# Streaming and retrieval attention with a two-layer MLP: the first two w_in loads divided, and the head of the written order changed

## The chip, the cores and the metric

The kernel runs on one core of one Trainium2 chip. The metric is device microseconds of one execution, given as the median of several runs. One execution was also taken with the hardware profiler; all views of the trace are of that one.

## What is computed

Four batches, eight heads, 768 positions, head width 64. Heads 0, 2 and 6 see every earlier key (retrieval heads); the others see the first 4 keys and a window of 64 (streaming heads). The 3072 x 512 result goes through a product with w_in (512 x 2048), a leaky ramp with a slope per column, and a product with w_out (2048 x 512).

```python
scores = scale * np.matmul(q, k.transpose(0, 1, 3, 2))
...
scores = np.where(mask[None, :, :, :], scores, -1000000000.0)
scores = scores - np.max(scores, axis=-1, keepdims=True)
a = np.exp(scores)
a = a / (np.sum(a, axis=-1, keepdims=True) + 1e-09)
return np.matmul(a, v).astype(np.float32)
...
h = x @ w_in
g = np.maximum(h, 0.0) + alpha * np.minimum(h, 0.0)
return (g @ w_out).astype(np.float32)
```

## The kernel before

The work is cut into about 1200 named pieces. A list, ORDER, written out at the top of the file, gives the order in which the pieces are recorded. Each engine does its instructions in that order, and so do the two engines that ask for transfers: SP for the rows of q, k and v, POOL for the weights and most of the results. A piece that waits holds back everything behind it on its engine. Nothing is scheduled at run time.

Heads come in pairs, `PAIRS = [(2, 6), (1, 5), (0, 4), (3, 7)]`, and a pair of one batch is a segment n, 0 to 15. The names of a segment's pieces:

- Lq, Lk, Lv: the loads of its rows (lines 239, 253, 276 and, for the small tail of a streaming head's v, 281), on SP, into buffers that are used in turn. One load moves 0.39 MB in one to three transfers. A transfer also waits until the transfer eight places before it on these queues has landed.
- Cq, Ck, Cv: casts to bf16 (lines 350 and 354, 363, 385 and 390), for the first segments on POOL, which is also the engine that asks for the weights.
- Tq, Tk: six transposes each on PE (line 405, for the first half of segment 0 line 403); tq, tk: the copies out of PSUM, on ACT or DVE.
- S: a block of scores on PE (lines 455, 504, 543), s: its exponentials on ACT (L511 for retrieval heads, L565 for streaming heads), m: masks on DVE. The score blocks of the first four segments take turns on two pairs of PSUM banks, so a block waits for the exponentials of the block before last.
- A: probabilities times values on PE (line 594), a: division on DVE (lines 604 and 605); X, x: transposes and copies into xT, the input of the MLP.

The MLP goes over eight token ranges t. P is a block of the first product (line 639), p and g the ramp (lines 644 and 651), O and Q blocks of the second product (lines 659 and 717), D, Z and b the sums around them. For t = 0 the blocks P0.0 to P0.5 are cut in three by the input pairs: part 0 takes the pairs that segments 0 and 1 fill, part 1 the pair of segment 2, part 2 that of segment 3:

```python
for part, cs in enumerate((range(0, 2), range(2, 3), range(3, 4))):
    item(f"P0.{f}.{part}", P1, 0, f, cs, LEAD)
```

The weights are loaded by POOL, which casts on the way. wi0 to wi7 (line 818) each bring a quarter of the columns of w_in for 64 of the 128 partitions, all four input pairs; wi0 and wi1 hold the columns of P0.0 to P0.3, wi2 and wi3 those of f 4 to 7, and so on. wo0 to wo3 (line 822) bring w_out.

warm0 to warm8 are matmuls on a tile of zeros (line 813), 32, 3, 14 and otherwise 4 of them, that fill PE while it has nothing to do.

Of the kernel before, what the change touches and what calls it, by code (L numbers as in the profile page):

```python
# [83 lines left out]
def kernel(  # L84
# [138 lines left out]
    def dram(t, offset, dims):  # L223
        return bass.AP(t.tensor, t.offset + offset, dims)
# [66 lines left out]
    nmr = const.tile([128, 5, 144], bf16, name="nmr")  # L291
    nms = const.tile([128, 192], bf16, name="nms")
# [5 lines left out]
    w_in_b = wpool.tile([128, 4, d_ff], bf16, name="w_in_b")  # L298
# [23 lines left out]
    def item(name, fn, *args):  # L322
        I[name] = lambda: fn(*args)
# [367 lines left out]
    for t, u in UNITS:  # L691
# [3 lines left out]
        S1 = owns[UNITS.index((t, u)) % 2 if t >= 2 else 0]  # L695
# [114 lines left out]
    def warm(n):  # L810
# [2 lines left out]
            nc.tensor.matmul(bank(got[0])[:, 0:128], busy, busy, start=True, stop=True)  # L813
        give(got)

    def load_w_in(n):
        hh, lo = n % 2, n // 2 * 512
        nc.gpsimd.dma_start(w_in_b[D * hh:D * hh + D, :, lo:lo + 512],
                            dram(moe_w_in, 4 * D * hh * d_ff + lo, [[d_ff, D], [D * d_ff, 4], [1, 512]]))
# [6 lines left out]
    def fill(name, ap, value, eng=nc.vector):  # L826
        item(name, eng.memset, ap, value)
# [159 lines left out]
```

## Time and profile before

| | |
|---|---|
| median of 3 runs | 224.23 us (223.76 to 226.41) |
| the profiled execution | 225.82 us, span of its instructions 224.1 us |
| PE busy | 214.4 us, 96% of the span |
| DVE, ACT, POOL busy | 183.5, 145.4, 45.0 us |
| moved by DMA | 35.98 MB, 161 GB/s over the span |

Times in the trace count from the start of the span, in microseconds. A row of the timeline gives the start, the duration, the engine, the line, the operation, out and in, how many instructions are merged in the row, and in brackets how long the engine had been idle and what released it. Where a wait is for several things at once, the row names only the one that came last by the profile. A row of the busy time by stretch gives, after the stretch and its length, the busy time of PE, PEld, DVE, ACT and POOL with the number of instructions, the granted TensorE clock, the mean share of the DMA engines in use (over 1 where two queues overlap) and GB/s. A DMA queue's row gives packets, MB and the share of the time of 16 engines.

### The profile page before, as it was taken

The page shows a single profiled execution, that of the slowest core. Times are in us where ns is not written, and L with a number is a line of the kernel's source. Part 1 is how long each engine was busy: PE and PEld are TensorE (multiplying, and loading weights), DVE is VectorE, ACT ScalarE, POOL GpSimd, SP SyncE. Part 2 cuts the span into 40 slices and gives each one's busy share as a digit, 9 for nine tenths or more (in the row PEclk, how much of TensorE's full clock was granted, in tenths as well). Part 3 has the DMA queues.
Part 4 walks back from the last instruction along what each step waited for, and adds up shares of the span by engine and source line. Part 5 has one row for each costly group of instructions (what it writes and reads, how often), then busy time and mean ns, then how long its engine had stood idle before and what let it go on. Part 6 is the DMA issues. An engine that isn't in the chain of part 4 may idle for free.

```text
span 224.1 us, 5705 instructions
## 1 busy us (share of the span) xinstructions
PE 214.4 (96%) x2169; PEld 155.3 (69%) x2186; DVE 183.5 (82%) x464; ACT 145.4 (65%) x311; POOL 45.0 (20%) x90
## 2 busy tenths in 40 slices
PE   8889879999999999999999999999999999999993
PEld 7769755656556654557899757757889955588882
DVE  6859655978778769999999996999999847799761
ACT  5879547989888869677861346789784136653430
POOL 6659673250322010030001110020000010000000
PEclk9999999999999999999999999999999999999999
DMA  6999999999999999999993699686002431100034
GB/s 184 316 218 208 287 241 226 234 206 189 205 253 229 173 247 219 196 219 205 220 191 86 140 286 155 144 131 125 4 0 105 83 113 47 47 3 0 3 140 143
DMA packets 89624, 35.98 MB, mean 161 GB/s; under 512 B 76645, under 2 KB 87933, under 8 KB 89597
## 3 DMA queue, kind: packets, MB, share of 16 engines
q1 hardware_dynamic: 83484, 26.35, 57.2%
q0 software_dynamic: 5792, 8.93, 17.2%
q8 instruction: 17, 0.28, 0.5%
q10 hardware_dynamic: 320, 0.34, 0.5%
q14 instruction: 11, 0.08, 0.1%
HBM read 27.58 MB, written 6.29 MB: 151 GB/s over the span
## 4 chain that ended last, share of the span: by engine, by line
PE 72%; DVE 9%; DMA 8%; POOL 4%; issue 3%; ACT 2%; SPq 0%; DVEq 0%; POOLq 0%
PE P L639 33%; PE P L717 21%; PE P L659 8%; PE P L594 5%; DMA rows<-in_q_dram 4%; DMA rows<-in_k_dram 4%; DVE g L651 3%; PE P L472 2%; PE P L465 1%; DVE g L702 1%; ACT eR L511 1%; PE P L405 1%; DVE eR L521 1%; POOL g L363 1%; POOL vb L390 1%
## 5 line engine op out<-in xcount | busy, mean ns | idle before, releaser
L639 PE MATMUL P<-xT,w_in_b 128*128 128x256 bf16 (+1 forms) x501 | 87.8, 325 | 1.6 <-DVE xn L605 1.0
L651 DVE SCALAR_TENSOR_TENSOR g<-neg,oma,P 128x256 bf16<-128x256 f32 (+1 forms) x128 | 71.4, 608 | 14.3 <-ACT neg L644 13.8
L639 PEld LDWEIGHTS <-w_in_b 128*128 128x128 bf16 x512 | 48.9, 98 | 31.6 <-issue 1.7
L644 ACT ACTIVATE neg<-P 128x512 f32<-128x512 f32 x96 | 55.3, 606 | 22.0 <-PE P L639 11.5
L717 PEld LDWEIGHTS <-g 128*128 128x128 bf16 x432 | 41.4, 98 | 6.2 <-DVE g L702 0.2
L511 ACT ACTIVATE eR<-P 128x448 bf16<-128x448 f32 (+4 forms) x63 | 37.1, 627 | 4.2 <-PE P L504 2.6
L717 PE MATMUL P<-w_out_b,g 128*128 128x256 bf16 x288 | 35.5, 273 | 0.0
L735 POOL DMA_DIRECT2D out_dram<-ot x12 | 7.2, 604 | 88.3 <-ACT ot L759 31.0
L659 PE MATMUL P<-w_out_b,g 128*128 128x512 bf16 x90 | 22.6, 380 | 0.3
L559 ACT ACTIVATE eS<-P 128x352 bf16<-128x352 f32 x45 | 20.7, 492 | 2.7 <-PE P L472 1.7
L605 DVE TENSOR_TENSOR xn<-P,rcp 128x448 bf16<-128x448 f32 (+1 forms) x32 | 19.5, 608 | 1.1
L570 DVE TENSOR_TENSOR eS<-eS,ms_near 128x352 bf16<-128x352 bf16 x45 | 14.7, 335 | 0.5 <-ACT eS L559 0.4
L659 PEld LDWEIGHTS <-g 128*128 128x128 bf16 x96 | 8.6, 98 | 9.1 <-issue 0.8
L702 DVE TENSOR_TENSOR g<-g 128x1024 bf16<-128x1024 bf16 x18 | 12.3, 686 | 0.1
L521 DVE TENSOR_TENSOR eR<-eR,mr_near 128x128 bf16<-128x128 bf16 (+5 forms) x54 | 10.9, 225 | 1.4 <-ACT eR L511 1.4
L455 PE MATMUL P<-qT,kT 128*128 128x192 bf16 (+14 forms) x68 | 11.1, 251 | 0.2 <-ACT eS L565 0.2
L594 PEld LDWEIGHTS <-eS 128*128 128x128 bf16 x260 | 9.9, 97 | 1.8
L594 PE MATMUL P<-vb,eS 128*128 128x65 bf16 x260 | 10.7, 193 | 0.0
L472 PE MATMUL P<-qT,kT 64*128 64x176 bf16 (+11 forms) x160 | 10.6, 250 | 0.0
L472 PEld LDWEIGHTS <-kT 64*128 64x128 bf16 x160 | 6.5, 94 | 5.7 <-issue 5.1
L594 PE MATMUL P<-vb,eR 128*128 128x65 bf16 x276 | 10.1, 193 | 0.0
L594 PEld LDWEIGHTS <-eR 128*128 128x128 bf16 x276 | 9.5, 97 | 0.5
(125 smaller groups left out, 263.0 us busy)
## 6 DMA issues: line engine op xcount, KB each, us to landing
out_dram<-ot POOLq DMA_DIRECT2D x18, 256.0 KB, 3.5
rows<-in_k_dram SPq DMA_DIRECT2D x21, 192.0 KB
rows<-in_q_dram SPq DMA_DIRECT2D x18, 192.0 KB
rows<-in_v_dram SPq DMA_DIRECT2D x17, 192.0 KB
rows<-in_v_dram SPq DMA_DIRECT2D x14, 196.0 KB
rows<-in_q_dram SPq DMA_DIRECT2D x7, 384.0 KB
w_in_b<-in_moe_w_in_dram POOLq DMA_DIRECT2D x8, 256.0 KB, 10.1
w_out_b<-in_moe_w_out_dram POOLq DMA_DIRECT2D x4, 512.0 KB, 13.8
```

Of the source, the lines that this page charges most:

```text
L472: nc.tensor.matmul(to, keys[own], queries[own], start=True, stop=True)
L511: nc.scalar.activation(ebuf[n, hh][:, lo:hi].rearrange("p (x c) -> p x c", x=len(parts)), P[:, got[0]:got[0] + len(parts), 0:(hi - lo) // ...
L559: nc.scalar.activation(slots, sc[:, 0:352].rearrange("p (s c) -> p s c", c=176), AF.Exp, scale=scale)
L570: nc.vector.tensor_tensor(slots, slots, ms_near[:, 0:2, :] if m == 0 else ms_near[:, 1:3, :], op=ALU.mult)
L594: nc.tensor.matmul(pav[:, i, :], e[:, o:o + 128], vv[:, j, hh, 0:D + 1], start=(m == 0), stop=(m == len(terms) - 1))
L605: nc.vector.tensor_tensor(xn[n][:, 0:nt, D * hh:D * hh + D], pav[:, :, 0:D], rcp.to_broadcast([128, nt, D]), op=ALU.mult)
L639: nc.tensor.matmul(psg[:, w * i:w * (i + 1)], w_in_b[:, c, 128 * fb:128 * (fb + 1)], xT[:, c, o:o + w], start=(x == 0), stop=(x == 3))
L644: nc.scalar.activation(neg[t, f], bank(held["P", t, f][0]), AF.Relu, scale=-1.0)
L651: nc.vector.scalar_tensor_tensor(g_buf[t % 2][:, fb, 0:w], neg[t, f][:, c], oma[:, fb:fb + 1], bank(got[0])[:, c], op0=ALU.mult, op1=ALU.add)
L659: nc.tensor.matmul(bank(held["O", t, s][0]), g_buf[t % 2][:, f, 128 * s:128 * (s + 1)], w_out_b[:, f, :], start=(f == 0), stop=(f == 15))
L702: nc.vector.tensor_tensor(to, x0, x1, op=op)
L717: nc.tensor.matmul(q_bank(t, u, CHAIN[y]), left[t, u][y][:, f, :], right[y][:, f, :], start=(first and f == 0), stop=(f == 7), skip_group_ ...
```

## The change

wi0 and wi1 are each divided in two. Part a brings the input pairs 1 and 2 (those of segments 1 and 0), part b the pairs 0 and 3; together they bring the same bytes to the same place. The pieces from about the 21st to the 356th of ORDER stand in another order; the first 20 or so and everything from S4.0.2 on stand as before. No other piece is added or taken out. The instructions of PE are the same in number and kind.

What moves on the engines, as far as it is spoken of below:

- PE: the scores of segment 0 now follow Tk1 and Tq1; warm2 (14 matmuls) moves from behind Tk0.0 to ahead of S0.1.2; Tq2 and Tk2 no longer stand side by side; Tk4 moves ahead of Tq5, and Tq4 behind X3 and P0.1.1, P0.2.1, P0.0.1; Tk5 moves ahead of S4.0.5 and P0.11.
- SP: Lv1 moves ahead of Lk3, Lk4 ahead of Lq5, Lk5 and Lq7 ahead of Lk6 and Lq6.
- POOL: wi1a behind Ck0.1, then Ck2.0, Cv0, Ck2.1, then wi0a, wi1b and wi6 ahead of Cq2; wi0b between Ck3.0 and Ck3.1; wi7, wi5 and wi3 behind Cv2; Ck4.0 and Ck4.1 both ahead of Cq4; wo0 behind Ck5.0, then the mask near_r (nr), then Ck5.1, and the other w_out loads behind that.
- ACT: alpha's load (La) ahead of the first half of Lk0.

```diff
@@ -12,23 +12,23 @@
 ...
-busy zero id warm0 kz3 Lq0.0 sz1 vz2 nms nmr so1 vz0 Lq0.1 Lk1 warm8 warm5 warm3 kz1 qz0 one Lq1 Lk0 La Ck0.0 kz2
-Cq0.0 Tq0.0 tq0.0 Tk0.0 qz warm2 Lk2 kz0 tk0.0 Ck1.0 Ck1.1 Cq0.1 Tk1 S0.0.1 s0.0.1 Tq0.1 S0.0.0 Cq1 warm7 Lv0 tk1.0
-sz2 vz1 vz3 Tq1 Lq2 Ck0.1 S0.0.2 s0.0.0 tk1.1 Tk0.1 Ck2.1 tq1 S1.1.0 s0.0.2 Ck2.0 warm4 tq0.1 s1.1.0 Cq2 tk0.1 Cv0 Lk3
-S0.1.0 kfz0 Lv1 vo ro0 Ck3.1 s0.1.0 Lq3 Ck3.0 wi1 wi0 Cq3 sz0 idf S1.0.0 so2 Al s1.0.0 so0 al S0.1.1 s0.1.1 Lv2 Tq2
-Tk2 tk2.1 tk2.0 S0.1.2 S1.0.1 A0.0 s0.1.2 a0.0 Cv1 A0.1 a0.1 Cv2 s1.0.1 tq2 S1.1.1 Tk3 S2.0.1 tk3.0 s1.1.1 S2.0.2 X0
-s2.0.1 x0 wi6 s2.0.2 wi7 Lv3 Lq5 Tq3 tk3.1 S2.0.0 wi5 m4.0.2 warm6 S2.1.0 A1.0 a1.0 Lk4 tq3 A1.1 Cv3.0 s2.0.0 Lq4 Lk6
-Lq6 Lk5 wi4 Cq5 a1.1 S3.0.0 s2.1.0 A2.0 s3.0.0 X1 x1 S3.0.1 S3.1.1 Ck4.0 P0.2.0 s3.0.1 A3.0 a2.0 Lq7 a3.0 S2.1.1
-s3.1.1 wi2 s2.1.1 Cv3.1 S3.1.0 wi3 A2.1 Cq4 wo1 s3.1.0 P0.1.0 P0.3.0 A3.1 Lk7 P0.0.0 Tq5 a2.1 tq5 X2 a3.1 Ck4.1 X3 Tq4
-Lv5 tq4 Tk4 x2 P0.2.1 Lv6 P0.1.1 tk4.0 P0.3.1 P0.0.1 x3 tk4.1 P0.13 p0.13 P0.0.2 P0.1.2 wo0 p0.0 P0.3.2 g0.0 P0.14
-g0.13 P1.14 wo3 p0.1 p1.14 g0.1 P1.2 p1.2 P0.8 Lv4 g1.14 Ck6.0 P0.9 g1.2 Cq6 m8.0.2 p0.8 nr p0.9 g0.8 m12.1.2 p0.3
-near0 near2 P0.15 S4.0.5 p0.14 P1.10 s4.0.5 Ck6.1 P0.11 P0.2.2 g0.9 Ck5.1 g0.14 p0.15 p1.10 P1.0 Lq8 Tq6 ro1 Ck5.0
-g0.15 p0.2 g0.3 S4.1.0 g1.10 wo2 p0.11 P1.12 P1.8 P0.7 g0.2 Lk8 s4.1.0 kfz1 g0.11 Lk9 p1.0 P0.5.0 p1.12 tq6 g1.0
-P0.5.1 Tk5 P0.4.0 p1.8 P0.6 tk5.0 g1.12 Lv7 p0.6 P0.10 g1.8 g0.6 P0.12 S4.0.3 P0.4.1 tk5.1 Cq7 s4.0.3 P0.4.2 D1.0
...
+busy zero id warm0 kz3 Lq0.0 sz1 vz2 nms nmr so1 vz0 Lq0.1 Lk1 warm8 warm5 warm3 kz1 qz0 one Ck1.0 Lq1 La idf Ck1.1
+Lk0 Cq0.0 vz1 Ck0.0 Lk2 Tq0.0 Tk0.0 kz2 Cq0.1 vo kz0 m12.1.2 tq0.0 Cq1 tk0.0 Tk1 Ck0.1 Tq1 S0.0.0 qz Lv0 wi1a Ck2.0
+s0.0.0 Tq0.1 Al warm7 tq1 S0.0.1 Cv0 Lq2 s0.0.1 Lv1 tk1.0 S0.0.2 Ck2.1 wi0a tk1.1 Tk0.1 tq0.1 S1.1.0 tk0.1 wi1b Tk2
+s0.0.2 s1.1.0 Lk3 wi6 S0.1.0 warm6 S1.0.0 Lq3 tk2.1 Cq2 s0.1.0 s1.0.0 Cv1 S0.1.1 s0.1.1 sz2 warm2 ro0 S0.1.2 s0.1.2
+vz3 Tq2 tk2.0 Ck3.0 S1.0.1 A0.0 S1.1.1 s1.0.1 tq2 al sz0 wi0b A0.1 so0 a0.0 S2.0.1 Lv2 Ck3.1 Cq3 Cv2 warm4 a0.1 Tk3
+s1.1.1 S2.0.2 Lv3 s2.0.1 X0 Tq3 tk3.0 Lk4 s2.0.2 x0 tk3.1 Lq5 wi7 S2.0.0 A1.1 tq3 A1.0 S2.1.0 s2.0.0 S3.0.0 a1.0 wi5
+a1.1 A2.0 X1 Lq4 ro1 wi3 s2.1.0 x1 Lk5 s3.0.0 Cv3.0 S3.0.1 Lq7 a2.0 Lk6 Lq6 S3.1.1 P0.3.0 s3.0.1 S2.1.1 A3.0 wi4 Cv3.1
+so2 a3.0 s3.1.1 Cq5 Ck4.0 S3.1.0 Ck4.1 P0.1.0 s2.1.1 A2.1 a2.1 m4.1.2 s3.1.0 m8.0.2 P0.2.0 A3.1 kfz2 P0.0.0 wi2 Cq4
+Lk7 X2 Tk4 a3.1 Tq5 x2 near0 X3 near2 tk4.0 tk4.1 Ck5.0 P0.1.1 P0.2.1 Lv6 Lv4 Lv5 P0.0.1 x3 Tq4 P0.1.2 P0.13 wo0 Lq8
+nr P0.0.2 tq5 tq4 P0.3.1 p0.1 P0.3.2 P0.14 Ck5.1 kfz1 p0.0 P0.2.2 P1.2 p0.14 g0.0 P1.14 Tk5 g0.1 g0.14 p0.13 S4.0.5
+wo2 P0.11 p1.2 g1.2 p0.3 tk5.0 p1.14 P1.0 g0.3 s4.0.5 p0.11 P0.9 g1.14 P0.8 g0.13 tk5.1 g0.11 p0.9 P1.10 S4.1.0 wo1
+P0.7 g0.9 p0.2 P0.15 p0.8 Lk8 p1.0 s4.1.0 wo3 g0.2 g0.8 P0.5.0 p1.10 g1.0 p0.15 Lv7 g1.10 P0.10 ns S5.1.1 g0.15 P1.12
+P0.4.0 S4.0.1 near1 m4.1.0 p0.7 P0.4.1 s5.1.1 p0.10 D1.0 S4.1.3 p1.12 P0.4.2 s4.0.1 g0.7 p0.4 P1.8 g1.12 m4.0.1 kfz0
+g0.4 p1.8 m4.0.2 g0.10 Ck6.1 Lk9 S5.1.2 P0.5.1 P0.12 s5.1.2 m5.1.2 P0.6 S5.0.1 p0.12 P0.5.2 s4.1.3 O0.1.0 p0.6 Cq7
...
@@ -813,6 +813,11 @@
             nc.tensor.matmul(bank(got[0])[:, 0:128], busy, busy, start=True, stop=True)
         give(got)
 
+    def load_w_half(n, part):
+        first = (1, 0)[part]
+        nc.gpsimd.dma_start(w_in_b[D * n:D * n + D, first:4 - first:(1, 3)[part], 0:512],
+                            dram(moe_w_in, (4 * n + first) * D * d_ff, [[d_ff, D], [(1, 3)[part] * D * d_ff, 2], [1, 512]]))
+
     def load_w_in(n):
         hh, lo = n % 2, n // 2 * 512
         nc.gpsimd.dma_start(w_in_b[D * hh:D * hh + D, :, lo:lo + 512],
@@ -861,7 +866,11 @@
         item(f"near{i}", to_near, i)
     for i in range(4):
         for x in range(i, 8, 4):
-            item(f"wi{x}", load_w_in, x)
+            if x < 2:
+                for part in range(2):
+                    item(f"wi{x}{'ab'[part]}", load_w_half, x, part)
+            else:
+                item(f"wi{x}", load_w_in, x)
         item(f"wo{i}", load_w_out, i)
         fill(f"kfz{i}", kf[i][:, 6, :, :], 0.0, nc.gpsimd)
     fill("nz0", NATK[0].bitcast(fp32), 0.0, nc.gpsimd)
```

More of the change, by code (lines that the diff above doesn't have):

```diff
@@ L25 @@
-near0 near2 P0.15 S4.0.5 p0.14 P1.10 s4.0.5 Ck6.1 P0.11 P0.2.2 g0.9 Ck5.1 g0.14 p0.15 p1.10 P1.0 Lq8 Tq6 ro1 Ck5.0
-g0.15 p0.2 g0.3 S4.1.0 g1.10 wo2 p0.11 P1.12 P1.8 P0.7 g0.2 Lk8 s4.1.0 kfz1 g0.11 Lk9 p1.0 P0.5.0 p1.12 tq6 g1.0
-P0.5.1 Tk5 P0.4.0 p1.8 P0.6 tk5.0 g1.12 Lv7 p0.6 P0.10 g1.8 g0.6 P0.12 S4.0.3 P0.4.1 tk5.1 Cq7 s4.0.3 P0.4.2 D1.0
-p0.10 D1.1 P0.5.2 S4.0.1 p0.5 O0.0.0 g0.10 P1.4 s4.0.1 P1.6 p0.4 near1 g0.5 g0.4 S4.1.3 p0.7 p1.6 m4.0.3 g0.7 s4.1.3
-p1.4 O0.1.0 g1.6 O0.0.1 S5.1.2 ns S4.0.0 g1.4 O0.1.1 p0.12 s5.1.2 g0.12 S4.1.1 S5.0.1 m5.1.2 s4.0.0 m4.0.1 S5.0.0
@@ L30 @@
-S4.1.4 S5.1.1 S4.0.4 O0.0.2 s5.0.1 s4.0.4 Cv6 S5.1.0 S5.0.2 Ck7.1 s4.1.4 m4.0.0 s5.1.1 Tk6 O0.2.0 m4.1.0 Cv5 kfz2
-tk6.1 O0.0.3 O0.1.2 Ck7.0 s5.1.0 m5.1.1 O0.1.3 m4.1.2 Cq8 m5.0.1 s5.0.0 Ck8 tk6.0 Cv4 m5.1.0 O0.2.1 m5.0.0 o0.0 S4.0.2
+busy zero id warm0 kz3 Lq0.0 sz1 vz2 nms nmr so1 vz0 Lq0.1 Lk1 warm8 warm5 warm3 kz1 qz0 one Ck1.0 Lq1 La idf Ck1.1
+Lk0 Cq0.0 vz1 Ck0.0 Lk2 Tq0.0 Tk0.0 kz2 Cq0.1 vo kz0 m12.1.2 tq0.0 Cq1 tk0.0 Tk1 Ck0.1 Tq1 S0.0.0 qz Lv0 wi1a Ck2.0
+s0.0.0 Tq0.1 Al warm7 tq1 S0.0.1 Cv0 Lq2 s0.0.1 Lv1 tk1.0 S0.0.2 Ck2.1 wi0a tk1.1 Tk0.1 tq0.1 S1.1.0 tk0.1 wi1b Tk2
@@ L32 @@
+g0.4 p1.8 m4.0.2 g0.10 Ck6.1 Lk9 S5.1.2 P0.5.1 P0.12 s5.1.2 m5.1.2 P0.6 S5.0.1 p0.12 P0.5.2 s4.1.3 O0.1.0 p0.6 Cq7
+P1.6 Ck6.0 s5.0.1 g0.6 Cv4 S5.0.0 Tk6 Ck7.0 p0.5 g0.12 O0.0.0 p1.6 Cq6 g1.8 P1.4 g0.5 s5.0.0 Ck7.1 tk6.1 O0.0.1 Tq6
+S5.1.0 tq6 S4.0.0 O0.1.1 g1.6 s5.1.0 O0.0.2 Cv6 tk6.0 m5.1.1 p1.4 Cq8 S4.0.3 S4.1.1 S4.0.4 S4.1.4 O0.0.3 s4.0.4 S5.0.2
+O0.1.2 s4.1.4 D1.1 s4.0.3 s4.0.0 m5.0.1 O0.1.3 m4.0.3 g1.4 Cv5 m4.0.0 Ck8 O0.2.0 m5.1.0 O0.2.1 m5.0.0 o0.0 S4.0.2
 S6.0.2 m4.1.4 S4.1.5 S6.1.0 s4.1.1 S6.0.5 o0.1 S6.1.2 m4.0.5 s5.0.2 S4.1.2 s4.0.2 s4.1.5 D2.1 s6.1.0 Lq9 O0.2.2 m4.0.4
```

## The prediction

> **What bounds the kernel now.** I read the page's engine totals and its chain first, then the busy time by stretch, then each wait of PE ahead of 35 us, then what those waits hang on.
>
> ```profile
> PE 214.4 (96%) x2169; PEld 155.3 (69%) x2186; DVE 183.5 (82%) x464; ACT 145.4 (65%) x311; POOL 45.0 (20%) x90
> PEclk9999999999999999999999999999999999999999
> PE 72%; DVE 9%; DMA 8%; POOL 4%; issue 3%; ACT 2%; SPq 0%; DVEq 0%; POOLq 0%
> ```
> ```profile
> 5.00:10.00 5.00, 4.58 (x66) 3.85 (x66) 4.16 (x12) 4.00 (x5) 3.26 (x7) 1.00 1.11 304
> 10.00:15.00 5.00, 3.86 (x44) 3.04 (x44) 2.91 (x12) 4.38 (x6) 1.77 (x3) 1.00 0.96 233
> 25.00:30.00 5.00, 4.16 (x67) 3.48 (x70) 3.67 (x9) 1.75 (x4) 3.89 (x7) 1.00 1.16 275
> 30.00:35.00 5.00, 3.51 (x37) 2.23 (x35) 1.23 (x3) 3.17 (x4) 4.26 (x6) 1.00 1.18 240
> 100.00:150.00 50.00, 49.79 (x494) 36.96 (x497) 47.52 (x113) 30.27 (x73) 4.22 (x7) 1.00 0.89 174
> 200.00:224.10 24.10, 20.45 (x187) 17.88 (x184) 15.94 (x34) 7.16 (x20) 0.00 (x0) 1.00 0.18 66
> ```
> PE is the bound: full from 35 us to 200 us, with room only in the head and in the tail. The tail's pieces keep their order, and the change adds no PE instruction. So whatever it does is decided by PE's waits in the first 35 us, and by new ones behind them. These are the old ones:
>
> ```profile
> 6.87 0.51 PE L405 MATMUL P<-ident,g 128*128 128x128 bf16 x6 [0.18 <-POOL g L363]
> 10.23 0.49 PE L405 MATMUL P<-ident,g 128*128 128x128 bf16 x6 [0.47 <-DVE kT L436]
> 12.28 0.24 PE L455 MATMUL P<-qT,kT 128*128 128x192 bf16 x1 [0.16 <-ACT eS L565]
> 14.55 0.84 PE L405 MATMUL P<-ident,g 128*128 128x128 bf16 x12 [0.75 <-POOL g L350]
> 25.78 0.38 PE L639 MATMUL P<-xT,w_in_b 128*128 128x512 bf16 x1 [0.96 <-DVE xn L605]
> 31.63 0.51 PE L405 MATMUL P<-ident,natq 128*128 128x128 bf16 x6 [0.77 <-POOL natq L350]
> 32.85 0.51 PE L405 MATMUL P<-ident,natk 128*128 128x128 bf16 x6 [0.72 <-POOL natk L363]
> ```
> They add up to 4.0 us. Even if all of them went and nothing new came, the time would fall by 4.0 of 224.2 us, under the 2% that a measurement of this kernel can about tell from no change.
>
> **The change part by part.** Sums go against the profiled execution's 225.82 us (span 224.1), 1.59 us above the median of the runs; I move the result by that.
>
> *Scores begin later: +1.05 us at PE.* In the new order PE makes Tk1, then Tq1, and only then the first score block S0.0.0; warm2, which filled the place, stands later.
>
> ```profile
> 7.71 0.83 POOL L350 CAST g<-rows 128x768 bf16<-128x768 f32 x1 [0.44 <-DMA rows<-in_q_dram]
> 8.48 0.39 PE L813 MATMUL P<-busy 128*128 128x128 bf16 x4
> 8.70 0.50 PE L405 MATMUL P<-ident,g 128*128 128x128 bf16 x6
> 9.04 0.35 PE L455 MATMUL P<-qT,kT 128*128 128x128 bf16 x2
> 7.99 0.35 PE L455 MATMUL P<-qT,kT 128*128 128x448 bf16 x1
> 7.85 1.75 ACT L511 ACTIVATE eR<-P 128x896 bf16<-128x896 f32 x2 [1.00 <-PE P L504]
> 15.99 0.92 ACT L511 ACTIVATE eR<-P 128x896 bf16<-128x896 f32 x1 [1.23 <-PE P L504]
> ```
> Tq1 needs the cast that ends at 7.71+0.83 = 8.54. Six transposes hold PE 9.04-8.70 = 0.34, a block of S0 8.48-7.99 = 0.49 and a drain of about 0.1, so the first exponentials start at about 9.5 instead of 7.85: ACT is 1.65 late. From there to s0.1.2 ACT has the same nine instructions; before, it had 1.23 of wait and more among them (s0.1.2 ends at 15.99+0.92 = 16.9), in the new order I count 0.5, so it ends at 17.4. PE's S0.1.2 ends at about 16.5 (S0.1.1 at 15.15, warm2's fourteen at 0.056, then 0.55) against 15.79. Tq2 (0.34) and warm4 (0.22) are then still to do, warm6 (0.22) is done: 0.71+0.34+0.22-0.22 = +1.05. Bounds 0.5 (ACT recovers all it can) to 1.65.
>
> *Three waits go: -2.9 us.* 0.96 for the first weights, 0.77 for Tq4, 0.72 for Tk4, and with each about 0.16, since a transpose's record lasts 0.22 where the next follows after 0.056.
>
> ```profile
> L818 POOL DMA_DIRECT2D w_in_b<-in_moe_w_in_dram x2: 642/708/773, 16.4 to 17.1; - x2
> DMA to landing us min/median/max: 6.6/7.4/8.3
> 30.74 0.83 POOL L350 CAST natq<-rows 128x768 bf16<-128x768 f32 x1 [1.64 <-DMA rows<-in_q_dram]
> 31.51 0.77 POOL L822 DMA_DIRECT2D w_out_b<-in_moe_w_out_dram x1
> 32.28 0.52 POOL L363 CAST natk<-rows 128x384 bf16<-128x384 f32 x1
> ```
> The second weight load was asked for at 17.1 and lands 8.3 later, at 25.4, the matmul runs at 25.78: the row names DVE, but the weights fit. Asked for at about 9 and 12.5, the halves with pairs 1 and 2 are there long before the first L639, now P0.3.0 at about 25.5 to 27. Tk4 waited on POOL because Ck4.1 stood behind Cq4's wait and a w_out issue; now it stands ahead of both. Tq4 now follows Tk4 and three more matmuls (1.0 us of work), and by the sum of the pieces is reached at 31.6 if nothing else is late, just when a cast like the old one (30.74+0.83) ends.
>
> *The weights take the rows' engines: +1.6 us, bounds 0 and 2.6.*
>
> ```profile
> q1 hardware_dynamic: 4503, 2.43, 111.2%
> q0 software_dynamic: 1172, 1.13, 74.5%
> q1 hardware_dynamic: 1167, 1.00, 42.8%
> 10.77 3.16 SPq L281 DMA_DIRECT2D rows<-in_v_dram x1
> 13.97 0.38 SPq L239 DMA_DIRECT2D rows<-in_q_dram x1
> 15.46 0.96 POOL L363 CAST g<-rows 128x384 bf16<-128x384 f32 x2
> 17.74 0.85 POOL L350 CAST g<-rows 128x768 bf16<-128x768 f32 x1
> ```
> The first line is the queue view of 5 to 13 us, rows alone: 304 KB per us. The next two are of 27 to 36 us, weights beside them: the packets go one for one (1172 to 1167), and the rows fall to 111 KB per us while a weight load of 0.26 MB takes 2.1 us. So a weight load ahead of a row transfer costs it 2.1 x (1-111/304) = 1.3 us, a half 0.65. Now k3: before, it was issued ahead of the blocked SP instruction (L281, until 13.93) and cast at 15.46 to 16.4 with no wait. Now Lv1 with that L281 stands ahead of Lk3, and wi1a, wi0a, wi1b and wi6 are asked for before about 14.3. Lower bound: k3 lands by the old rate, one row load (1.3) and three halves (1.95) later, 18.7, one cast 19.2, in time for Tk3, which the order reaches at 19.5: 0. Upper: it is issued as q3 was (13.97, cast at 17.74, 3.8 later), plus two and a half weight loads 3.3, so 21.0, second cast 21.6: 2.1; with q3 behind it 0.5 more. I take 1.6, nearer the upper, since k3 really stands behind the L281.
>
> *k5: +0.4 us, bounds 0 and 1.5.* Tk5 moves up to about 4.5 us behind Tq4 (some 38 us); k5 is now the load behind q4, and its second cast stands behind a w_out issue (0.77) and the mask near_r (1.28). Beside the weights its 0.39 MB take 3.5 us more than q4: about 38. That cover gone, DVE and the POOL issues behind Ck5 are late too.
>
> *Priced at nothing.* Two more weight issues on POOL (0.64 each) come by 14.3, ahead of Cq2; Tq2 is wanted only at 16.5 now. That is also why the 0.75 wait of Tq2 does not return; it is contained in the 1.05. alpha's DMA ahead of Lk0 on ACT delays the k0 cast by 0.45, behind Tq0.0's six transposes. Lk2 waits as much longer, but SP soon blocks at Lq2 anyway. From 35 us on the same work is reordered under a full PE; w_out is asked for later, but its first user, the P2 block, comes at 52 us.
>
> Sum: +1.05 -2.9 +1.6 +0.4 = +0.15, taken as +0.2: 226.0 of span and launch, **224.4 us** beside the median: no change.
>
> **The rivals.** *Rows in time (faster, 222.4).* k3 and k5 are on time, both terms 0: 1.05-2.9 = -1.85. For it: the old DMA engines had a hole that early weights can fill for nothing:
>
> ```profile
> 14.00:15.40 1.40, 0.85 (x14) 0.84 (x15) 0.00 (x0) 0.76 (x1) 1.40 (x3) 1.00 0.46 57
> ```
> Against: k3's place behind L281.
>
> *q4 starved (slower, 227.2).* Its load took 9.88 us already.
>
> ```profile
> 20.81 9.88 DMA rows<-in_q_dram
> ```
> The weight queue starts some 7 us earlier and can by then have moved 7 x 0.126 = 0.88 MB more, 3.4 loads at 1.3 = 4.4 us: q4 lands at 35.1, its cast ends at 35.95 and Tq4 starts 4.35 after its 31.6. That takes k3's place in the sum: 1.05-2.9+4.35+0.4 = +2.9. It decides once q4 lands after about 32.3. Against: the last five weight loads stand behind Cv2 and Cv3.0 in POOL's order as before, so they start no earlier.
>
> *The first weights were not the wait (225.5).* Then DVE's xn was, 0.96+0.16 stay: +1.1. Against: xn was done at 25.5, and nothing of P0 reads it.
>
> *PE's clock falls back (225.9).* From the last warm matmul at about 5 us to S0.0.0 at 8.9 PE has only 24 transposes. If the clock halved, some 2 us of matmuls would double, about 1.5 us of it not hidden behind ACT. Against:
>
> ```profile
> 29.70:33.20 3.50, 2.01 (x34) 1.67 (x32) 1.53 (x3) 1.60 (x2) 2.46 (x4) 1.00 1.17 241
> 33.20 1.03 PE L639 MATMUL P<-xT,w_in_b 128*128 128x512 bf16 x4
> ```
> Here PE made transposes alone for 3.5 us, 2.01 of it busy, and the four matmuls after it stand (1.03-0.38)/3 = 0.22 apart, full rate. [...]
>
> **How the numbers follow.** Forecast (223.3 to 225.9) 0.42; rows in time 0.22; q4 starved 0.20; weights not the wait 0.10; clock 0.06. The likeliest is 224.4. The range takes the first rival's centre at the low end and the second's at the high end: 222.2 to 227.3. Faster by over 2% (below 219.7) needs more than all old waits together: 0.02. Slower by over 2% (above 228.7) is the far half of the starved case with a further stall behind it: 0.08. Within: 0.90.
>
> **What would show it.** Right: first L511 on ACT at about 9.5; no wait ahead of the first L639; a wait of PE of 1 to 2 us at the transposes near 20 us, released by POOL's L363 behind a k row; none or a short one for Tq4; a short one at about 38 us. If PE's idle time ahead of 35 us is under 2.5 us, the rows were in time; if the longest wait is for natq near 33 us, q4 was starved; if L813 or the scores at 9 us run at half rate, the clock. A new PE wait behind 40 us, where I count none, makes the prediction wrong, as does a first L639 that still waits.

## The result: a little slower, by 1%

The changed kernel takes 227.41 us (median of 22 runs, 225.5 to 229.62) beside 225.21 us for the kernel before on the same chip (22 runs). The ratio is 1.0096, 95% interval 1.0072 to 1.012: about 2.2 us were lost, where the forecast had +0.2, and 227.41 lies just above its range of 222.2 to 227.3. The loss is under 2% and clear of the noise. Medians are of all executions of a kernel, and ratios leave out those more than 1.5% above its fastest, so the two can differ a little. (The forecast's 224.4 stood beside 224.23, the median of the first three executions of the kernel before.)

The first profiled execution of the changed kernel took 228.96 us and had a lower granted clock (mean 0.992), so the readings below are from another execution of the same kernel, 227.04 us, clock 1.00 throughout (the run c_again). It stands beside the profiled execution of the kernel before, 225.82 us, so this pair of traces shows 1.2 us of the loss. Its page, engine totals, clock and the shares of the chain:

```profile
PE 215.0 (95%) x2169; PEld 155.5 (69%) x2186; DVE 183.1 (81%) x464; ACT 145.7 (65%) x311; POOL 47.1 (21%) x92
PEclk9999999999999999999999999999999999999999
PE 69%; DMA 12%; DVE 9%; SPq 3%; issue 2%; ACT 2%; POOL 2%; ACTq 0%; DVEq 0%; POOLq 0%
```

PE has the same 2169 instructions. Its share of the chain fell from 72% to 69% and the share of the DMA engines rose from 8% to 12%. Its waits of 0.15 us and more ahead of 45 us, from its timeline:

```profile
5.72 0.52 PE L403 MATMUL P<-ident,g 128*64 128x128 bf16 x6 [0.24 <-ACT g L363]
6.97 0.51 PE L405 MATMUL P<-ident,g 128*128 128x128 bf16 x6 [0.72 <-POOL g L363]
8.85 0.51 PE L405 MATMUL P<-ident,g 128*128 128x128 bf16 x6 [1.37 <-POOL g L350]
10.86 0.54 PE L455 MATMUL P<-qT,kT 128*128 128x448 bf16 x3 [0.18 <-ACT eR L511]
20.18 0.51 PE L405 MATMUL P<-ident,g 128*128 128x128 bf16 x6 [0.17 <-POOL g L363]
24.88 0.97 PE L594 MATMUL P<-vb,eR 128*128 128x65 bf16 x27 [0.25 <-POOL vb L390]
28.13 0.49 PE L594 MATMUL P<-vb,eS 128*128 128x65 bf16 x11 [0.26 <-POOL vb L341]
39.89 4.51 PE L639 MATMUL P<-xT,w_in_b 128*128 128x512 bf16 x27 [1.01 <-DMA w_in_b<-in_moe_w_in_dram]
```

They add up to 4.2 us; the seven of before made 4.0. The three that the forecast struck out are gone: the first L639 (26.99), Tk4 and Tq4 (31.59 to 33.3) start without a wait. In their place stand a longer head, two short waits for values and 1.01 us for weights at 39.89, at a place where before had none. The chain of the same run says where that one comes from:

```profile
12.59 0.47 SPq L276
13.11 10.68 DMA rows<-in_v_dram
23.89 0.95 POOL vb L390
25.80 1.23 POOL w_in_b L823 x2
27.03 0.57 POOL vb L385
28.03 11.81 DMA w_in_b<-in_moe_w_in_dram
39.89 0.39 PE P L639
```

Read downwards: SP asks for v2 at 12.59, sooner than in the kernel before (14.40), but the second of its transfers takes 10.68 us, with weights asked for ahead of it (the first at 9.19) and beside it (the last at 13.86); POOL stands 2.85 us at the cast Cv2, until 23.89; behind Cv2 in POOL's order are the last five weight loads, asked for from 25.2 on; the fourth of them, wi4, is asked for at 28.03 and lands at 39.85, and PE waits for it at P0.11. In the kernel before the same cast ran at 20.11 and the same issues at 21.39:

```profile
20.11 0.92 POOL L390 CAST vb<-rows 128x896 bf16<-128x896 f32 x1
21.39 1.84 POOL L818 DMA_DIRECT2D w_in_b<-in_moe_w_in_dram  x3
```

So asking for the first weights 7 us earlier made the cast of v2 3.8 us later and with it four of the last five weight loads (wi4 28.03 against 26.06). The order of the loads counts as well. The kernel before asks for wi4 ahead of wi2 and wi3; wi4 lands at 36.18, 2.0 us ahead of P0.8 (38.18), the first block that needs it. The changed order asks for wi3 ahead of wi4, although P0.7, the first block that needs wi3, comes 4.5 us behind P0.11 (44.43; wi3 landed at 37.62). Meanwhile SP, which loads the rows, stood 5.45 us at the issue of v3 in the changed kernel, against 1.32 us before:

```profile
16.90 5.45 SPq L276 DMA_DIRECT2D rows<-in_v_dram  x2
```

and the DMA engines were not kept full. Busy time by stretch, 20 to 25 us, the last two columns being the share of the DMA engines and GB/s, the changed kernel:

```profile
20.00:25.00 5.00, 4.58 (x79) 4.17 (x79) 4.31 (x12) 4.34 (x6) 2.00 (x4) 1.00 0.81 167
```

and the kernel before:

```profile
20.00:25.00 5.00, 4.82 (x97) 4.56 (x95) 3.88 (x11) 4.00 (x7) 3.17 (x6) 1.00 1.15 230
```

### The profile page after: what moved, and what is told of

Its sections match the earlier page's. It is cut to its first block, busy times and chain, and to the rows that moved or that the text cites. A ratio compares the mean times of both kernels' runs of the same rounds, so it can differ in the third digit from the quotient of the medians.

```text
span 227.2 us, 5709 instructions
## 1 busy us (share of the span) xinstructions
PE 217.0 (96%) x2169; PEld 157.3 (69%) x2186; DVE 183.1 (81%) x464; ACT 145.6 (64%) x311; POOL 46.5 (20%) x92
## 4 chain that ended last, share of the span: by engine, by line
PE 66%; DMA 13%; DVE 9%; SPq 6%; issue 2%; POOL 2%; ACT 0%; ACTq 0%; DVEq 0%; POOLq 0%
PE P L639 30%; PE P L717 21%; PE P L659 7%; DMA w_in_b<-in_moe_w_in_dram 5%; DMA rows<-in_v_dram 4%; PE P L594 4%; SPq L276 3%; DVE g L651 3%; DMA xT<-xn 2%; PE P L472 2%; DMA rows<-in_k_dram 2%; PE P L465 1%; SPq L239 1%; DVE g L702 1%; DVE eR L521 1%
## 5 line engine op out<-in xcount | busy, mean ns | idle before, releaser
L639 PE MATMUL P<-xT,w_in_b 128*128 128x256 bf16 (+1 forms) x501 | 88.7, 325 | 1.9 <-DMA w_in_b<-in_moe_w_in_dram 1.3
L651 DVE SCALAR_TENSOR_TENSOR g<-neg,oma,P 128x512 bf16<-128x512 f32 (+1 forms) x128 | 71.8, 608 | 12.8 <-ACT neg L644 11.9
L639 PEld LDWEIGHTS <-w_in_b 128*128 128x128 bf16 x512 | 48.8, 98 | 32.2 <-DMA w_in_b<-in_moe_w_in_dram 1.6
L455 PE MATMUL P<-qT,kT 128*128 128x192 bf16 (+14 forms) x68 | 12.0, 262 | 0.2
L472 PE MATMUL P<-qT,kT 64*128 64x176 bf16 (+10 forms) x156 | 10.4, 251 | 0.4 <-DMA kT<-natk 0.4
```

Source lines behind the costliest of these rows:

```text
L472: nc.tensor.matmul(to, keys[own], queries[own], start=True, stop=True)
L639: nc.tensor.matmul(psg[:, w * i:w * (i + 1)], w_in_b[:, c, 128 * fb:128 * (fb + 1)], xT[:, c, o:o + w], start=(x == 0), stop=(x == 3))
L651: nc.vector.scalar_tensor_tensor(g_buf[t % 2][:, fb, 0:w], neg[t, f][:, c], oma[:, fb:fb + 1], bank(got[0])[:, c], op0=ALU.mult, op1=ALU.add)
```

## The experiments

Ratios are to the kernel before, timed on the same chip, with 95% intervals. The edits move names in ORDER and nothing else, except where a run says otherwise.

**The changed kernel again**, twice, for traces.

> The changed kernel, unaltered, for a second trace. Three causes are in dispute. Late scores: the first exponentials on ACT start about 3 us later than before (11.05 against 7.85), about 2 us of which stays. Late weights: the early weight halves delay v2 (24.6 against 19.1 us), so POOL asks for the last five weight loads 3 to 4 us later and PE waits 1.3 us at 41 us. Clock: PE idles 2 us ahead of the first scores and the granted clock falls to 0.50 from 9.4 to 12.7 us, 1.7 us of clock lost. If the clock is the cause, an execution with the clock at 1.00 throughout is about as fast as before (ratio 1.00); if the other two are, it stays at 1.009 to 1.010 and the wait at 41 us is there with the clock at 1.00 too.

Measured: 226.95 us (12 runs), ratio 1.0081 [1.0054, 1.0109]. The clock fell in this trace too (to 0.50, from 8.9 to 12.3 us) and its span was still only 225.0 us; wi4 landed at 37.87 and PE came to P0.11 at 39.46, so that it did not wait for weights. Over 34 executions of the changed kernel the mean clock was under 0.995 in 7, over 95 of the kernel before in 16; the medians of the others are 227.15 and 225.22 us. The clock is not the difference.

> The changed kernel, unaltered, for a third trace, since the second one showed no wait at 41 us. Late weights: v2 lands at 22 us or later again and the waits that follow differ from run to run (values at 27 to 30 us, natk or natq at 33 to 35, weights at 38 to 41), 0.3 to 2.8 us together; time 226.5 to 227.8. If the early weights did nothing, v2 would land by 20 us and no such wait would be there.

Measured: 227.04 us with the clock at 1.00, the trace shown above. The 1.01 and 0.51 us of new waits are in the expected range.

**Scores first.**

```diff
-Tk1 Ck0.1 Tq1 S0.0.0 qz Lv0
+Tk1 Ck0.1 S0.0.0 Tq1 qz Lv0
```

> The transposes of q1 stand behind the first score block S0.0.0 instead of ahead of it; all else as in the changed kernel. Late scores: the first exponentials start at about 8.4 us instead of 11.05, and 1.5 to 2 us of the loss comes back: ratio to before 1.000 to 1.003. Late weights: the wait at 41 us is still there, grows by what PE gained ahead of it, and the ratio stays at 1.008 to 1.010. Clock: PE's longest idle stretch ahead of 10 us shrinks from 1.25 to about 0.9 us; if that keeps the clock at 1.00, ratio 1.003 in runs that had it low and no change in the others.

Measured: 227.26 us, 1.0089 [1.0056, 1.0122]. The first exponentials came at 8.81 us, 1.1 earlier than in c_again, and no gain can be measured: in the trace PE stands at P0.11 for 0.50 us, until 38.26, and wi4 lands at 38.22. The late scores are not the cause.

**Weights late.**

```diff
-... wi1a Ck2.0 ... wi0a ... wi1b ... wi6 ... wi0b ... Ck3.1 Cq3 Cv2 ... wi7
+... Ck2.0 ... Ck3.1 wi1a wi1b wi0a wi0b Cq3 Cv2 ... wi6 wi7
```

> The changed kernel with the four halves asked for together behind Ck3.1 and the third weight load behind Cv2, about where the kernel before asks for its first two and its third. Late weights: v2 and v3 land by about 20 and 25 us, the wait at 41 us (1.34) and the one for the values at 29 us (0.26) go, but the first L639 may wait up to 1 us for its weights again; ratio 1.003 to 1.007. Late scores: nothing of the 2 us comes back, ratio 1.008 to 1.012 (the more if the first weights are waited for).

Measured: 225.52 us, 1.0017 [0.9991, 1.0043]. Five weight transfers moved back on POOL take away most of the loss: 1.4 us less than the changed kernel in the same comparison. The ratio lies a little below the range of the first reading. The stretch of 20 to 25 us is full again:

```profile
20.00:25.00 5.00, 5.00 (x101) 4.62 (x99) 4.58 (x13) 4.69 (x6) 4.87 (x10) 1.00 1.03 227
```

and the chain reaches the weights sooner, the cast of v2 at 20.26 and the wait at their end 0.23 us (chain, then timeline):

```profile
20.26 0.87 POOL vb L390
21.54 2.41 POOL w_in_b L823 x4
24.87 12.85 DMA w_in_b<-in_moe_w_in_dram
37.76 0.39 PE P L639
37.76 4.51 PE L639 MATMUL P<-xT,w_in_b 128*128 128x512 bf16 x27 [0.23 <-DMA w_in_b<-in_moe_w_in_dram]
```

**Filler into the hole.**

```diff
-Tk1 Ck0.1 Tq1 ... S0.1.1 s0.1.1 sz2 warm2
+Tk1 Ck0.1 warm2 Tq1 ... S0.1.1 s0.1.1 sz2
```

> The changed kernel with the fourteen warm-up matmuls of warm2 moved from behind S0.1.1 to between the transposes of k1 and of q1, into PE's idle stretch of 8 to 9.2 us. Clock: the granted clock stays at 1.00 in every run, the mean falls to the level of the runs with clock 1.00, ratio 1.005 to 1.008 (about 227.4 less 0.3 to 1.0). Late scores: PE is held at most 0.1 us longer ahead of Tq1, and the removed filler at 17 us stood under ACT's work: ratio 1.009 to 1.010. Late weights: the same, the wait at 41 us stays.

Measured: 227.78 us, 1.011 [1.0066, 1.0155]; mean clock 0.999 or 1.0 in all six executions. That is a little above the ranges given; with the clock up in all of them nothing was gained.

**Both: weights late and scores first.**

> The changed kernel with both edits of the first runs: the halves asked for behind Ck3.1 and the third weight load behind Cv2, and the first score block ahead of the transposes of q1. Late weights alone: the same as with the weights alone put back, ratio 1.000 to 1.003, because the head's lateness was never the bound. Late scores as well: with the transfers on time the first exponentials at 8.4 instead of about 9.5 us now count, and 0.7 to 1.5 us come back: ratio 0.995 to 0.998.

Measured: 226.14 us, 1.0037 [1.0003, 1.0071], above both forecast ranges. Again nothing from the scores. PE stood 0.66 us at the transposes of k2 at 12.8 instead, which led to the two runs at the end of this section.

**The other five weights ahead of Cv2.**

```diff
-Ck3.1 Cq3 Cv2 ... wi7 ... wi5 ... wi3 ... wi4 ... wi2
+Ck3.1 Cq3 wi7 wi5 wi3 wi4 wi2 Cv2
```

> The changed kernel with the last five weight loads (wi7, wi5, wi3, wi4, wi2) asked for ahead of the cast of v2, while POOL waits for v2's rows; the early ones stay early. If the harm of the early weights goes by POOL's order (v2 late, so the last weights late, so PE waits for them at 37 to 41 us), these now land by about 36 us, no L639 waits for them, and the ratio falls to 1.002 to 1.005. If it goes by the rows themselves (every row load behind a weight is late: the values for L594, then k4 and q4), v2 and v3 land later still, PE waits for vb and for natk or natq, and the ratio rises to 1.012 to 1.025.

Measured: 231.59 us, 1.0188 [1.0119, 1.0257]. Of the two readings the second held. PE no longer waits for weights; it waits for rows:

```profile
28.80 0.22 PE L594 MATMUL P<-vb,eS 128*128 128x65 bf16 x2 [1.43 <-POOL vb L385]
34.86 0.51 PE L405 MATMUL P<-ident,natk 128*128 128x128 bf16 x6 [2.04 <-POOL natk L363]
```

**Early weights in the kernel before.** Whole loads, its own order:

```diff
-Cq1 ... Ck0.1 ... Ck2.1 ... Ck2.0 ... Ck3.0 wi1 wi0 Cq3 ... x0 wi6 s2.0.2 wi7
+Cq1 ... Ck0.1 wi1 ... Ck2.1 ... Ck2.0 wi0 wi6 ... Ck3.0 Cq3 ... x0 s2.0.2 wi7
```

> The kernel before, whole loads and its own order, with only the first three weight loads (wi1, wi0, wi6) asked for early, behind Ck0.1 and Ck2.0, at about 9 and 10.5 us. Late weights: v2 lands at 22 us or later instead of 19.1, its cast and the weights behind it on POOL are 3 us late, and although the wait of 0.96 us for the first weights goes, the ratio is 1.004 to 1.010. Late scores: the head is that of before, so the 0.96 us is gained and the ratio is 0.995 to 0.998.

Measured: 228.71 us, 1.0175 [1.0115, 1.0235]. Here the row load that stands behind the weights is q3, which PE wants at once:

```profile
22.54 0.60 PE L405 MATMUL P<-ident,g 128*128 128x128 bf16 x6 [3.14 <-POOL g L350]
```

With early weights the changed order loses 1% and the old order 1.75%. The rest of the changed order seems to take part of the harm away, but the two intervals touch (up to 1.012, from 1.0115).

**Undivided.** wi1 where wi1a stood, wi0 where wi0a stood, the b halves left out, the loads as in the kernel before.

> The changed kernel with the first two loads of w_in whole: wi1 where wi1a stood, wi0 where wi0a stood, nothing where the b halves stood. If the division does harm or good by itself (two more issues on POOL of 0.6 us each, smaller loads), the ratio moves off that of the changed kernel by 0.003 or more; if only the bytes ahead of v2 count (0.78 MB instead of 0.65 by the time v2 is asked for), it stays at 1.008 to 1.012.

Measured: 227.92 us, 1.0103 [1.007, 1.0137]. The division does nothing that can be measured.

**How many early.**

```diff
+ two halves early: wi1a wi0a as in the change; Ck3.1 wi1b wi0b; Cv2 ... wi6 wi7
+ four halves early: only wi6 moved, Cv2 ... wi6 wi7
```

> The changed kernel with two halves of the first weights early (wi1a, wi0a, 0.26 MB), wi1b and wi0b behind Ck3.1 and wi6 behind Cv2. If the bytes ahead of v2 and q3 set the loss (0 early: 1.0017, 0.78 MB: 1.009), a third of them gives about 1.004; if any early weight does the whole harm, 1.008 to 1.010; if the first halves only fill holes of the DMA engines, 1.001 to 1.002.

> The changed kernel with all four halves early and only wi6 (0.26 MB) back behind Cv2. Two thirds of the early bytes: about 1.006 by the bytes; 1.008 to 1.010 if wi6 does nothing; near 1.002 if wi6 alone, which nobody needs before 33 us, is the harm.

Measured, beside the ends:

| early weights | us | ratio |
| --- | --- | --- |
| none | 225.52 | 1.0017 [0.9991, 1.0043] |
| 0.26 MB | 226.34 | 1.0047 [1.0024, 1.007] |
| 0.52 MB | 227.06 | 1.0087 [1.0052, 1.0122] |
| 0.78 MB (the change) | 226.95 | 1.0081 [1.0054, 1.0109] |

By the medians the first two steps are 0.7 to 0.8 us each, as by the bytes; the last, wi6, costs nothing more. Neighbouring intervals overlap; only the first row stands clear of the last two. In the profiled executions wi4 landed at 37.71, 37.51 and 41.06 us in the first three rows, and at 41.12, 37.87 and 39.85 in the three of the change.

**One wait of the kernel before by itself.**

```diff
-A2.1 Cq4 wo1 ... a3.1 Ck4.1 X3 Tq4
+A2.1 Ck4.1 Cq4 wo1 ... a3.1 X3 Tq4
```

> The kernel before with one cast moved: Ck4.1 ahead of Cq4 and the first w_out load on POOL. The part of the change that should have helped: the wait of 0.72 us for natk at 32.9 us goes, ratio 0.996 to 0.998. If PE's slack elsewhere swallows it, 0.999 to 1.001. The stretch of transposes and waits from 29.7 to 33.2 us shortens to about 2.7 us; if it is there that the clock falls in about one run in four of the kernel before (mean clock under 0.995), such runs become rare.

Measured: 225.38 us, 1.0014 [0.998, 1.0047], clock under 0.995 in 1 of 12 executions. A gain of 0.72 us would be 0.9968, outside the interval. In the trace the wait for k4 went, and PE waited as long for q4 instead (q4's load and cast from the chain, then PE):

```profile
21.20 10.80 DMA rows<-in_q_dram
32.06 0.84 POOL natq L350
32.95 0.51 PE L405 MATMUL P<-ident,natq 128*128 128x128 bf16 x6 [1.46 <-POOL natq L350]
33.29 0.50 PE L405 MATMUL P<-ident,natk 128*128 128x128 bf16 x6
```

1.46 in one place where 0.77 and 0.72 had stood. PE comes to q4 ahead of k4 in this order, so it was not the missing wait that brought it there sooner: q4's rows landed later than in the trace of the kernel before (a load of 10.80 us and not 9.88, a cast at 32.06 and not 30.74). Nothing ahead of that load had been moved; whether a typical execution does the same is not shown.

**The head again.** Weights late, Ck2.1 ahead of Cv0, without and with the scores first.

```diff
-Ck2.0 ... Cv0 ... Ck2.1
+Ck2.0 Ck2.1 ... Cv0
```

> The changed kernel with the weights late (halves behind Ck3.1, wi6 behind Cv2) and the second half of k2's cast, Ck2.1, directly behind Ck2.0, that is ahead of v0's cast Cv0. If PE's head is held by k2 standing behind v0 on POOL (its cast ran at 12.3 us, its rows had landed at 9.4), Tk2 comes 0.7 us earlier only if PE gets there earlier, and with Tq1 still ahead of the first score block it does not: 1.000 to 1.003. If neither matters, the same.

> The same with the first score block ahead of the transposes of q1 as well. If the two orders hold the head together, PE's wait of 0.66 us for k2 at 12.8 us goes and about 1 us of the head's lateness comes back: ratio 0.996 to 0.999, first exponentials at 8.3 to 8.8 us, no PE wait at 12 to 13 us. If the head's lateness is hidden or comes from elsewhere, 1.001 to 1.004 as with each alone.

Measured: 225.40 us, 1.0003 [0.9977, 1.003], and 226.00 us, 1.0037 [1.001, 1.0064]. In the second the head did come earlier, and PE then waited for the transfers:

```profile
20.61 0.51 PE L405 MATMUL P<-ident,g 128*128 128x128 bf16 x6 [0.37 <-POOL g L350]
26.27 0.38 PE L639 MATMUL P<-xT,w_in_b 128*128 128x512 bf16 x1 [0.66 <-DMA w_in_b<-in_moe_w_in_dram]
38.21 4.51 PE L639 MATMUL P<-xT,w_in_b 128*128 128x512 bf16 x27 [0.56 <-DMA w_in_b<-in_moe_w_in_dram]
```

The traces show where such gains end. The second column below is how much more time PE has lost by 20 us than in the kernel before: the time less the usual start-to-start distance of all matmuls begun by then (for each line and shape, the mean of the shortest third over all traces). From about 62 us on PE has the same instructions in the same order in all of these kernels, so the last two columns are read directly, from the start of the same matmul, at 62 us and at the last block of the MLP (at 217.67 in the kernel before).

| trace | lost more by 20 us | wi4 lands | P0.11 begins | its wait | behind at 62 us | behind at the last block |
| --- | --- | --- | --- | --- | --- | --- |
| changed (c_again) | 1.6 | 39.85 | 39.89 | 1.01 | 1.03 | 1.03 |
| weights late | 1.3 | 37.71 | 37.76 | 0.23 | -1.10 | -0.67 |
| weights late, scores first | 1.1 | 38.15 | 38.20 | 0.05 | -0.66 | 1.07 |
| weights late, k2 first | 0.7 | 37.60 | 37.65 | 0.73 | -1.21 | -0.84 |
| weights late, k2 and scores first | 0.4 | 38.16 | 38.21 | 0.56 | -0.65 | -0.41 |
| before, Ck4.1 moved | 0.2 | | | | 0.43 | 0.65 |

In ten of the thirteen traces that have the changed order or an edit of it, P0.11 begins 0.04 or 0.05 us after wi4 has landed. Of the four kernels with the weights late, the one with the shortest head is 0.9 us ahead of the first at 20 us and 0.45 behind it at 62: in these traces, what the head gains is given back to waits for rows and weights. Each row is one execution, and executions of one kernel differ by more than these differences. What is lost behind 62 us was not followed.

## Why the prediction was wrong, step by step

**"Scores begin later: +1.05"**: the size was about right, the meaning was not. The first exponentials came at 9.89 us (forecast 9.5), and with the weights late PE had lost 1.3 us more by 20 us. But three kernels that make the head earlier are no faster. What the head loses or gains does not reach the end.

**"Priced at nothing"** holds the step that failed: "From 35 us on the same work is reordered under a full PE". PE was not full there. The changed order asks for wi3 ahead of wi4, so wi4 lands a load later (2.2 us between the two in c_again), and with the early weights both are asked for later. PE stands at P0.11 until wi4 has landed: 1.01 us in c_again, 1.34 in the first trace, where the forecast counted no wait. Up to P0.11 the sum held: without that wait PE is level with the kernel before (1.03-1.01), and +0.15 was forecast. That was luck in part, as the head cost 1.6 and not 1.05, and k3 0.17 and not 1.6.

**"Three waits go: -2.9"** was therefore right as far as P0.11 and wrong as a gain of the whole. In the trace with the weights late PE goes from 1.3 us behind the kernel before at 20 us to 1.3 ahead on reaching P0.11 (-1.10-0.23), so 2.6 of the 2.9 came. The time did not follow: the ratio is 1.0017, +0.4 us (-0.2 to +1.0), where the forecast's terms without contention give 1.05-2.9 = -1.85. I took waits of PE as costs that can be struck out one by one. They were places where PE met a stream of row and weight transfers that keeps the DMA engines busy (1.08 to 1.21 of their time from 15 to 50 us in the kernel before), and what PE gained it could lose at the next thing that the stream brings. The profile had said so: the wait at 32.85 hung on a row load of 9.88 us, which I quoted and used only for a rival.

The waits for wi4 with the weights late (0.05 to 0.73) are only a part of the missing 2.2 us (from -1.85 to +0.4). Another part may be the reference: I took the waits of an execution of 225.82 us off a median that was 1.6 us lower, as if a median execution waited as long. No second trace of the kernel before shows how long it does wait; this part stays open.

**"The weights take the rows' engines: +1.6, and k5 +0.4"**: right in mechanism and nearly in size, wrong in place. Together 2.0 were forecast; the early weights cost 1.4 to 1.8 us (1.0081 or 1.0096 against 1.0017, times 225). But Tk3 waited 0.17, not 1.6, and Tk5 (38.19) not at all. I followed the load that moves behind a weight (k3) and not the one that then stands last, v2, whose cast has the other weight loads behind it on POOL. I even wrote that these five "start no earlier", as an argument against the starved q4, and did not ask if they start later, or which of them PE wants first.

**The rivals.** Rows in time: k5 was and k3 nearly (0.17), and the gain did not come. q4 starved: not in the change, where Tq4 does not wait; in the experiments with the other weights ahead of Cv2, k4 and q4 were starved as described, 2.04 us, because the condition named against it (the last five behind Cv2) was taken away. First weights not the wait: no, they were. In the kernel before the second load lands at 17.12+8.3 = 25.4, and PE's own load of the first of these weights, after 0.82 us of idle time, starts at 25.54. The clock: it did fall in the first trace of the changed kernel, which I had argued against; it is no part of the 1%, as the counts above show. That row of PEld, and the busy time by stretch of the first trace of the changed kernel:

```profile
25.54 0.13 PEld L639 LDWEIGHTS <-w_in_b 128*128 128x128 bf16 x2 [0.82 <-issue]
```
```profile
8.00:9.00 1.00, 0.00 (x0) 0.00 (x0) 0.97 (x3) 0.00 (x0) 0.64 (x1) 1.00 1.25 294
9.00:10.00 1.00, 0.76 (x7) 0.76 (x8) 0.99 (x3) 0.00 (x0) 1.00 (x3) 0.65 1.00 172
10.00:11.00 1.00, 1.00 (x8) 0.66 (x6) 0.28 (x3) 0.00 (x0) 0.87 (x2) 0.50 0.75 227
11.00:12.00 1.00, 1.00 (x11) 0.77 (x9) 0.00 (x0) 0.95 (x2) 0.67 (x1) 0.50 1.15 335
12.00:13.00 1.00, 1.00 (x10) 0.71 (x9) 0.00 (x0) 0.66 (x1) 1.00 (x3) 0.65 1.06 213
```

**The signs.** I had named a PE wait behind 40 us as what would make the prediction wrong; it ends at 39.89 in c_again and at 41.16 in the first trace.

**What stays open.** Why the waits differ so much between executions of one kernel (the weights were waited for in two of three traces of the changed kernel, and the trace of the undivided loads has 2.75 us for k4 instead). No run asks for wi4 ahead of wi3 in the changed order, which the landings above suggest. What order of rows and weights would shorten the stream itself is open too. No version tried is faster than the kernel before; the best, weights late with k2 first, is level with it.

## What to carry to other kernels

Before a wait of the bound engine is struck out, follow the chain behind it: if it ends in a queue that is busy for the whole stage, the gain can be lost at the next thing that the queue brings (with the weights late 2.6 us of waits went, and the time stood at +0.4). So list for every load of the stage when it is asked for, when it lands and which block wants it first, and do so for the new order too: a load asked for ahead of one that is wanted sooner shows at once. The early requests were paid here by what stood behind them: v2's second transfer took 10.68 us, and its cast ran at 23.89 and not at 20.11. POOL issues in order, its last five weight loads from 25.2 on behind that cast, so the price is found by walking on from the late load to its cast and to everything that is issued behind it. To price a moved transfer, vary how much of it is moved and take several executions of each: single traces differed too much to give the price (wi4 landed between 37.87 and 41.12 us in the three of the change).

## What the runs showed of the hardware

- The granted clock, where it fell in the midst of the work, fell to 0.50 and stayed there for about 3.4 us, in all five traces that show such a fall: from 9.3 to 12.7 us in the first trace of the changed kernel, 8.9 to 12.3 in the changed kernel again, 35.3 to 38.7 with the other weights ahead of Cv2, 22.8 to 26.2 with early weights in the kernel before, 36.2 to 39.7 undivided. In the rows above, of the first trace, it is 0.7 us of the stretch from 9 to 10 (half of it makes 0.65), all of 10 to 12, and 0.7 of 12 to 13. There it fell some 3.4 us after the last filler, a time in which PE had made eighteen transposes and waited; c_again, an execution of the same order, had no such fall. What makes the clock fall is not shown: in the quiet stretch that I quoted, from 29.7 to 33.2 us in the kernel before, PE made transposes and waited too (2.01 us busy of 3.50), and the clock stayed at 1.00. The fillers of that first trace:

```profile
1.06 4.87 PE L813 MATMUL P<-busy 128*128 128x128 bf16 x44 [1.06 <-DVE zero L323]
```

- Where the clock fell behind a long wait, the wait cost more than itself. In the kernel before with early weights, PE stood 3.14 us for q3, until 22.54, and from 22.8 on ran at 0.50 of the clock: score matmuls of 192 columns followed one another after 0.16 us (24.33 to 25.45), and after 0.08 when the clock was back (26.77 to 26.93). The mean clock was 0.983 to 0.992 in all six executions:

```profile
24.00:26.00 2.00, 2.00 (x20) 1.90 (x19) 0.00 (x0) 1.08 (x2) 1.94 (x5) 0.50 1.09 350
```
